# Opening and convolution of an S4 layer as one written list of single-engine steps: 24-step poles, loads on two queues, five forms of phase rounding

## The chip, the cores and the metric

The kernel runs on one core of a Trainium2 chip. A core has five engines that run their own instruction lists and wait for one another at semaphores: TensorE (PE, matrix products, results in PSUM), VectorE (DVE), ScalarE (ACT, functions from tables that must be loaded), GpSimd (POOL) and SyncE (SP). Transfers are started from an engine's list; here SP and POOL start nearly all of them. The metric is the device time of one execution in microseconds. The median of 3 runs of the kernel before is 1785.16 (1783.84 to 1787.31).

## The reference

One layer with a state-space convolution and one gated MLP, both modulated by a vector c; length 2048, 576 channels, 128 states per channel. Cut to what the change touches:

```
dt = exp(log_dt);  logdA = dt * (A_re + i A_im)
K[d, l] = Re sum_n C[d,n] * exp(logdA[d,n] * l) * dt*B[d,n]      # 2048 taps for 576 channels
y = (causal convolution of u with K over l) + u * Dskip
sa, ca, ga, sb, cb, gb = silu(c) @ w_mod
x = x + ga * y,   with u = layernorm(x) * (1 + ca) + sa
x = x + gb * mlp(layernorm(x) * (1 + cb) + sb)
```

## The kernel before

`body` (L120) calls `ssm` (L165), which does everything up to the first residual sum, then `phase_a` and `phase_b` of the MLP. The change is in `ssm`.

**Poles.** `poles` reads the seven pole arrays and computes decay, phase and amplitude of each pole; each is split into three bf16 parts and stored to `pa_d` and `pb_d` in DRAM. `p0` covers the first of four channel blocks (144 columns wide), `p1` the other three (432 wide). They are generators: each `next` issues one of seven pieces. `poles_load` reads a block back as the matmul operands `lb`, `lc`, `la` (two buffers each), from GpSimd's queue.

**Groups.** The kernel K is made in 36 groups of 16 channels, nine for each channel block. A group passes through

- `e_unit` (L444): exponents by matmul into PSUM (`ps` and `pk`), then ACT's Exp into `et` (L451, L454);
- `t_unit` (L458): phases in turns by matmul into a two-bank PSUM tile `ps` (L467), then the distance to the nearest whole turn into `ft`, and its absolute value (L484);
- `s_unit` (L487): ACT's sine of both, for cosine and sine (L489, L490);
- `p_unit` (L492): four products on DVE (L500 to L503);
- `kg_unit` and `k1_unit`: matmuls (L513, L530) and evacuations (L516, L535 on DVE, L537 on ACT).

Rounding has two forms. For groups under `NR = 10` PE adds a large constant and takes it off again by matmuls with constant rows of `sel`, and DVE copies the result out of PSUM (L479); for the others ACT adds the constant (L482) and DVE subtracts twice (L483):

```
if g < NR:  magics(2112, True); phases((768, 0), False, False)
            magics(2240, False); phases((1536, 1792), False, True)
            V.tensor_copy(f, pa)
else:       phases((768, 0), True, True)
            A.activation(f, pa, AF.Identity, bias=magic)
            V.scalar_tensor_tensor(f, f, MAGIC, pa, op0=ALU.subtract, op1=ALU.subtract)
```

PSUM holds two tiles `ps` of two banks (`ps2`, L182) and four tiles `pk` of one (`ps1`, L185). The first serve exponents, phases, modulation and layer norm; the others the rest.

**Layer norm and modulation.** `mod_unit` makes six rows from c and w_mod; `ln_load` brings x in four blocks into two buffers, `ln_stats` takes mean and variance (blocks 0 and 1 on ACT, 2 and 3 by bn_stats on DVE, L408), `ln_rows` and `ln_pair` normalise, take the first step of the transform over l, and store to `u1_d` by 16 transfers of GpSimd (L436).

**Convolution.** For each of five channel ranges: `u_unit` (transform, L580, and two transfers that swap halves, L582, L583), `z_unit` (kernel transform, L592, and product with u, L593), `v_unit` (inverse, L600 to L603, to `v_d`), `y_unit` (last inverse, residual sum and store, L646 to L649).

**What sets the order.** A loop over ticks 0 to 39 calls the units: in tick t group t makes its phases, t−1 its sines, t−2 its products, t−3 and t−4 the rest; exponents come for three groups in every third tick; the layer norm has ticks 0 to 7; pole reloads stand at ticks 7, 13 and 21; convolution steps are placed by the table `plan`. Within a queue the scheduler may reorder what the loop issues, except calls through `mlp.tied`, which stay in program order (L152 in the profile). The part behind the loop (L750 on: the last convolution steps beside the MLP's start) is written out by hand and pinned. Loads are on SP's queue; stores, swaps of u and pole reloads are on GpSimd's.

Of the kernel before, what the change touches and what calls it, by code (L numbers as in the profile page):

```python
# [18 lines left out]
D = 576  # L19
# [144 lines left out]

def ssm(tc, I, x1_d, consts_s, dram, mod_d, mlp):  # L165
    nc = tc.nc
# [4 lines left out]
    with ExitStack() as ctx:  # L171
# [24 lines left out]
        ep = early.enter_context(tc.tile_pool(name="ep", reuse_waits="tile", bufs=2, side="right"))  # L196


        def poles(c0, c1, Q, own=None):
            w = 144 * (c1 - c0)  # L200
            f0, f1 = CW * c0, CW * c1

            def t(n, dt=F32):
                return ep.tile([128, 432], dt, name="t_" + n, bufs=1)[:, :w]

            todo = []

            def split3(*items):

                n = 3 // (c1 - c0)  # L210
                parts = []
                for i, (src, dst, k) in enumerate(items):
                    if not todo:
                        t_ = ep.tile([128, 3, 432], BF, name="pt")
                        todo.extend(t_[:, :, w * j:w * j + w] for j in range(n))
                    parts.append((src, dst, k, todo.pop(0), t("sq%d" % (i % 2))))
                for src, dst, k, pt, q in parts:
# [3 lines left out]
                for src, dst, k, pt, q in parts:  # L221
                    V.tensor_tensor(pt[:, 2], q, pt[:, 1], op=ALU.subtract)
                    for c in range(c0, c1):
                        for h in range(2):
                            Q.dma_start(dst[c, h, k:k + 3].rearrange("q (p f) -> p q f", p=64),
                                        pt[64 * h:64 * h + 64, :, 144 * (c - c0):144 * (c - c0) + 144])

            nat = {}
            for n in ("log_dt", "A_im", "A_re", "C_re", "B_re", "C_im", "B_im"):
                nat[n] = t("n_" + n) if own is None else own[:, len(nat) * w:len(nat) * w + w]  # L230
                S.dma_start(nat[n].rearrange("p (c f) -> p c f", c=c1 - c0), I["A_" + n][f0:f1].rearrange("(c p f) -> p c f", p=128, f=144))

            def run():
                Cr, Ci, Br, Bi = nat["C_re"], nat["C_im"], nat["B_re"], nat["B_im"]
                wr, wi, q1, q2 = t("wr"), t("wi"), t("q1"), t("q2")
                ldt, dt, al, tau, tau64, rnd = nat["log_dt"], t("dt"), nat["A_re"], nat["A_im"], t("tau64"), t("rnd")
                A.activation(dt, ldt, AF.Exp)
                V.tensor_tensor(tau, dt, tau, op=ALU.mult)
                V.tensor_scalar(tau, tau, 1.0 / (2 * math.pi), 2097152.0, op0=ALU.mult, op1=ALU.min)
                V.tensor_scalar(tau, tau, -2097152.0, None, op0=ALU.max)  # L240
                V.tensor_scalar(rnd, tau, MAGIC, MAGIC, op0=ALU.add, op1=ALU.subtract)
                V.tensor_tensor(tau, tau, rnd, op=ALU.subtract)
                V.tensor_tensor(al, dt, al, op=ALU.mult)
                yield
                V.tensor_tensor(wr, Cr, Br, op=ALU.mult)
                V.tensor_tensor(wi, Ci, Br, op=ALU.mult)
                V.tensor_tensor(q1, Ci, Bi, op=ALU.mult)
                V.tensor_tensor(wr, wr, q1, op=ALU.subtract)
                V.tensor_tensor(q2, Cr, Bi, op=ALU.mult)
                V.tensor_tensor(wi, wi, q2, op=ALU.add)  # L250
                yield
                ax, ay, mx, mn, ph, lw = Cr, Ci, Br, Bi, t("ph"), t("lw")
                V.tensor_single_scalar(ax.bitcast(I32), wr.bitcast(I32), 0x7FFFFFFF, op=ALU.bitwise_and)
                V.tensor_single_scalar(ay.bitcast(I32), wi.bitcast(I32), 0x7FFFFFFF, op=ALU.bitwise_and)
                V.tensor_tensor(mx, ax, ay, op=ALU.max)
                V.tensor_tensor(mn, ax, ay, op=ALU.min)
                V.tensor_scalar(mx, mx, 1e-37, None, op0=ALU.max)
                V.reciprocal(rnd, mx)
                V.tensor_tensor(mn, mn, rnd, op=ALU.mult)
                yield  # L260
                A.activation(lw, mx, AF.Ln)
                AP = mlp.tied.scalar
                AP.activation(q1, mn, AF.Square)
                AP.activation(q1, q1, AF.Ln, bias=one)
                AP.activation(ph, mn, AF.Arctan)
                V.tensor_scalar(tau64, tau, 64.0, None, op0=ALU.mult)
                V.tensor_scalar(rnd, tau64, MAGIC, MAGIC, op0=ALU.add, op1=ALU.subtract)
                V.tensor_tensor(tau64, tau64, rnd, op=ALU.subtract)
                yield
                split3((al, pb_d, 0), (tau, pa_d, 0))  # L270
                yield
                V.scalar_tensor_tensor(lw, q1, 0.5, lw, op0=ALU.mult, op1=ALU.add)
                V.tensor_tensor(lw, lw, ldt, op=ALU.add)
                split3((tau64, pa_d, 3), (lw, pb_d, 3))
                yield
                V.tensor_scalar(ph, ph, 1.0 / (2 * math.pi), None, op0=ALU.mult)
                V.tensor_tensor(ax, ay, ax, op=ALU.is_gt)
                V.tensor_scalar(ay, ph, -2.0, 0.25, op0=ALU.mult, op1=ALU.add)
                V.tensor_tensor(ay, ay, ax, op=ALU.mult)
                V.tensor_tensor(ph, ph, ay, op=ALU.add)  # L280
                V.tensor_scalar(ay, ph, -2.0, 0.5, op0=ALU.mult, op1=ALU.add)
                V.scalar_tensor_tensor(ay, wr, 0.0, ay, op0=ALU.is_lt, op1=ALU.mult)
                V.tensor_tensor(ph, ph, ay, op=ALU.add)
                yield
                V.scalar_tensor_tensor(ay, wi, 0.0, ph, op0=ALU.is_lt, op1=ALU.mult)
                V.scalar_tensor_tensor(ph, ay, -2.0, ph, op0=ALU.mult, op1=ALU.add)
                V.scalar_tensor_tensor(ph, tau, 31.5, ph, op0=ALU.mult, op1=ALU.add)
                V.tensor_scalar(rnd, ph, MAGIC, MAGIC, op0=ALU.add, op1=ALU.subtract)
                V.tensor_tensor(ph, ph, rnd, op=ALU.subtract)
                split3((ph, pa_d, 6))  # L290

            return run()
# [3 lines left out]
        def poles_load(c, Q):  # L296
            for n, d_, k in (("lb", pb_d, 0), ("lc", pa_d, 0), ("la", pa_d, 3)):
                t_ = tb.tile([112, 9, 128], BF, name=n)
                if n == "lb":
                    Q.memset(t_[32:64], 0.0)  # L300
                for h in range(2):
                    Q.dma_start(t_[64 * h:64 * h + 48], d_[c, h, k:k + 6].rearrange("q (c g n) -> (q c) g n", c=8, g=9))
                lt[n, c] = t_
# [10 lines left out]

        def mod_init():
            A.activation(ec, cT, AF.Exp, scale=-1.0)
            V.tensor_scalar(ec, ec, 1.0, None, op0=ALU.add)
            V.reciprocal(ec, ec)
            V.tensor_tensor(ec, ec, cT, op=ALU.mult)

# [5 lines left out]
        def mod_load(k):  # L326
# [6 lines left out]
            for hh in range(2):  # L333
                S.dma_start(wmt[k][hh], I["w_mod"][:, k, hh])
# [5 lines left out]
        msk = cp.tile([128, 2], F32, name="msk")  # L340

        def mod_unit(k):
            wm = wmt.pop(k)
            mpart = ep.tile([128, D], F32, name="mpart", bufs=1)
            pm = ps2()
# [5 lines left out]
            A.activation(v3(mpart), pm[:, :, :HC], AF.Copy)  # L351
            pm = ps2()
            for hh in range(2):
                T.matmul(pm[:, hh, :HC], ones, mpart[:, HC * hh:HC * hh + HC], start=True, stop=True)
            src = pm[:, :, :HC]
            if k == 2:
                A.activation(v3(gar), src, AF.Copy)
            elif k == 1:
                V.scalar_tensor_tensor(v3(cga), src, 1.0, v3(gar), op0=ALU.add, op1=ALU.mult)
            elif k == 0:  # L360
                V.tensor_tensor(v3(sga), src, v3(gar), op=ALU.mult)
# [4 lines left out]
            else:  # L366
                mrow = ep.tile([128, D], F32, name="gar", bufs=1)
# [4 lines left out]
                G.dma_start(mod_d[k - 3:k - 2], mrow[0:1])  # L372


        x4s = {}
        r1t = {}

        def ln_load(i):
            x4s[i] = ep.tile([128, 4, D], F32, name="ln_x")
            S.dma_start(x4s[i], I["x"][:, 4 * i:4 * i + 4])  # L380
# [306 lines left out]
        for _ in range(3):  # L687
            next(p0)
# [1510 lines left out]
```

## Time and profile before

| | |
|---|---|
| median of 3 runs | 1785.16 us |
| span of the profiled execution | 1781.6 us |
| part of the span up to the end of the convolution | 456 us |
| PE, DVE, ACT, POOL busy, share of the span | 94%, 71%, 47%, 14% |
| first exponential on ACT begins | 46.41 us |
| last group's product on DVE ends | 381 us |
| last sum of the residual begins | 453.75 us |

Rows of the profile name a line of the kernel, an engine, an operation and "out<-in". In tables by stretch each engine has its busy microseconds in the stretch and a count of instructions; PEclk is the clock granted to TensorE as a share of the full one. In the timeline a row is start, duration, engine, line, operation, and in brackets the idle time before it and what ended it. In the chain of waits a row is start, length and what the end of the execution hung on then.

### The profile page before, as it was taken

The page shows a single profiled execution, that of the slowest core. Times are in us where ns is not written, and L with a number is a line of the kernel's source. Part 1 is how long each engine was busy: PE and PEld are TensorE (multiplying, and loading weights), DVE is VectorE, ACT ScalarE, POOL GpSimd, SP SyncE. Part 2 cuts the span into 40 slices and gives each one's busy share as a digit, 9 for nine tenths or more (in the row PEclk, how much of TensorE's full clock was granted, in tenths as well). Part 3 has the DMA queues.
Part 4 walks back from the last instruction along what each step waited for, and adds up shares of the span by engine and source line. Part 5 has one row for each costly group of instructions (what it writes and reads, how often), then busy time and mean ns, then how long its engine had stood idle before and what let it go on. Part 6 is the DMA issues. An engine that isn't in the chain of part 4 may idle for free.

```text
span 1781.6 us, 36375 instructions
## 1 busy us (share of the span) xinstructions
PE 1671.0 (94%) x15174; PEld 1242.2 (70%) x15174; DVE 1258.9 (71%) x2259; ACT 833.9 (47%) x1118; POOL 244.8 (14%) x400
## 2 busy tenths in 40 slices
PE   3687899997899999999999999999999999999999
PEld 1243555565455545777877888888888888888887
DVE  6874999965899998698899778688344478344432
ACT  4766998854477656445434444234232223122210
POOL 3312232333122211000000000000111100111100
PEclk9576999998899999999999999999999999999999
DMA  9456645579689879777675886874766573556531
GB/s 260 133 179 184 189 124 172 172 204 297 206 260 283 246 229 267 281 245 256 233 224 164 287 302 240 267 244 125 249 219 232 195 234 98 192 195 219 192 111 41
DMA packets 183381, 376.24 MB, mean 211 GB/s; under 512 B 39360, under 2 KB 103488, under 8 KB 182448
## 3 DMA queue, kind: packets, MB, share of 16 engines
q1 hardware_dynamic: 140416, 175.23, 32.7%
q0 software_dynamic: 36896, 172.01, 29.3%
q10 hardware_dynamic: 5904, 26.67, 3.7%
q8 instruction: 119, 1.95, 0.5%
q14 instruction: 46, 0.38, 0.1%
HBM read 263.11 MB, written 101.31 MB: 205 GB/s over the span
## 4 chain that ended last, share of the span: by engine, by line
PE 57%; DVE 16%; DMA 3%; issue 3%; ACT 1%; POOL 0%; ACTq 0%; SPq 0%; DVEq 0%; POOLq 0%
PE ps L152 54%; DVE bsz L152 2%; DVE zset L152 1%; DVE n L152 1%; DVE gt L152 1%; DVE rq L152 1%; DMA zset<-set_d 1%; DVE wsp L152 1%; DMA wsst<-in_w_spT 1%; DVE wso L152 1%; DVE nt L152 1%; DVE raw L152 1%; DVE rx L152 1%; DVE bsx L152 1%; DVE z L152 1%
## 5 line engine op out<-in xcount | busy, mean ns | idle before, releaser
L152 PEld LDWEIGHTS <-zset 128*128 128x128 f16 x7182 | 702.1, 98 | 91.9 <-DVE zset L152 7.6
L152 PE MATMUL ps<-wsp,zset 128*128 128x256 f16 x6048 | 667.4, 273 | 6.9 <-DVE zset L152 5.8
L152 PE MATMUL pz<-wz,nt 128*128 128x512 f16 (+1 forms) x1120 | 223.4, 360 | 8.9 <-DVE nt L152 4.2
L152 ACT ACTIVATE z<-gt 128x1024 f16<-128x1024 f32 x56 | 59.0, 1054 | 288.6 <-DVE gt L152 288.6
L152 PEld LDWEIGHTS <-nt 128*128 128x128 f16 x1120 | 109.9, 99 | 116.3 <-DVE nt L152 5.7
L152 DVE SCALAR_TENSOR_TENSOR gt<-ps,sc,bsp 128x512 f32<-128x512 f32 x36 | 27.0, 749 | 205.0 <-PE ps L152 203.3
L1907 POOL DMA_DIRECT2D zset<-set_d x96 | 50.8, 529 | 868.5 <-PE ps L152 614.6
L152 PE MATMUL ps<-wout,z 128*128 128x288 f16 x1344 | 170.0, 286 | 0.0
L152 PEld LDWEIGHTS <-z 128*128 128x128 f16 x1344 | 131.5, 98 | 33.0
L152 PE MATMUL ps<-n2o,zset 128*128 128x256 f16 x1134 | 128.2, 273 | 0.0
L152 DVE SCALAR_TENSOR_TENSOR gt<-ps,sc,gt 128x512 f32<-128x512 f32 (+1 forms) x180 | 122.2, 696 | 7.9 <-DVE gt L152 0.5
L152 DVE TENSOR_TENSOR raw<-raw 128x512 f32<-128x512 f32 (+2 forms) x228 | 119.1, 528 | 12.3 <-DMA raw<-z_d 7.9
L152 ACT ACTIVATE zset<-raw 128x1792 f16<-128x1792 f32 x48 | 81.0, 1690 | 57.8 <-PE ps L152 23.4
L152 DVE TENSOR_TENSOR zset<-raw,zset 128x1792 f16<-128x1792 f32 x48 | 96.9, 2019 | 14.9 <-ACT zset L152 14.9
L152 DVE TENSOR_TENSOR z<-ps,z 128x512 f32<-128x512 f32 (+1 forms) x126 | 71.9, 598 | 36.8 <-ACT z L152 26.7
L152 ACT ACTIVATE wsp<-raw,sc 128x1792 f16<-128x1792 f32 x25 | 44.6, 1785 | 43.0 <-DVE raw L152 35.3
L152 ACT ACTIVATE z<-z,sc 128x1024 f32<-128x1024 f32 x21 | 24.1, 1149 | 75.6 <-DVE z L152 71.9
L152 ACT ACTIVATE z<-pz,sc 128x512 f32<-128x512 f32 (+1 forms) x96 | 52.3, 579 | 15.0 <-PE pz L152 10.9
L152 PE MATMUL ps<-n2q,wf 128*128 128x512 f16 x252 | 55.7, 379 | 0.0
L152 ACT ACTIVATE z<-z,nm,r 128x1152 f32<-128x1152 f32 x24 | 31.5, 1343 | 50.3 <-DVE nm L152 28.2
L501 DVE TENSOR_TENSOR pg<-et,ft 128x1024 f32<-128x1024 f32 x36 | 43.8, 1217 | 13.3 <-ACT ft L489 11.6
L152 PE MATMUL ps<-wout,z1b 128*128 128x288 f16 x384 | 52.6, 286 | 0.5 <-ACT z1b L152 0.5
(358 smaller groups left out, 2461.9 us busy)
## 6 DMA issues: line engine op xcount, KB each, us to landing
zset<-set_d POOLq DMA_DIRECT2D x96, 896.0 KB, 4.9
raw<-z_d SPq DMA_DIRECT2D x48, 512.0 KB, 5.7
set_d<-zset ACTq DMA_DIRECT2D x24, 896.0 KB, 6.1
z_d<-z POOLq DMA_DIRECT2D x32, 576.0 KB, 9.2
zset<-wa_d POOLq DMA_DIRECT2D x18, 896.0 KB, 4.8
raw<-in_w_spT SPq DMA_DIRECT2D x25, 512.0 KB, 4.4
set_d<-zset SPq DMA_DIRECT2D x12, 896.0 KB, 5.9
u_d<-st1o POOLq DMA_DIRECT2D x16, 576.0 KB, 4.1
```

The source lines that it names most:

```text
L152: return self.tc.keep_in_program_order(f(*a, **k))
L501: V.tensor_tensor(pr, pi, c3[:, :, None, :].to_broadcast([128, 16, 2, 32]), op=ALU.mult)
L1907: self.nc.gpsimd.dma_start(o, self.set_d[f, j - 1] if j else self.wa_d[f])
```

## The change

`nc` in `ssm` is now `mlp.tied`, so that every instruction of the stage keeps the place in which it is written, on each engine. The units are cut into steps, as a rule of one engine each (`e_p` matmul, `e_a` exponential; `t_p` phases, `t_i` copy or added constant, `t_b` absolute value; `s_f`, `s_c` sines; `p_a`, `p_b`, `p_c` products; and so on), and one list calls them. The 24-piece poles, the layer norm's statistics (block 0 on ACT, blocks 1, 2 and 3 by bn_stats on DVE), the convolution and the hand-written part behind the loop are words of the same list. A table `GPQ` names 41 loads that go on GpSimd's queue; the rest stay on SP's. A table `MODE` gives each group's form of rounding, and `COPY` says for each group which engine evacuates `k1` (DVE 14 times; 13 before).

```diff
-    nc = tc.nc
+    nc = mlp.tied
+MODE = [int(k) for k in "333301130222221440204304000000000000"]
+COPY = "010001110000011111010000000100100011"
+ORDER = """
+pole_in.0.6 pole_in.0.5 pole_in.0.3 pole_in.0.0 pole_in.0.2 pole_in.0.4 pl.0.3 pole_in.0.1 pl.0.0 pole_in.1.1 pole_in.1.2 pole_in.1.5 load.c pl.0.4
...
+    def Q(*a):
+        return G if ".".join(str(k) for k in a) in GPQ else S
...
+    def t_p(g):
...
-            if g < NR:
+            if MODE[g]:
                 magics(2112, True)
                 phases((768, 0), False, False)
                 magics(2240, False)
                 phases((1536, 1792), False, True)
-                V.tensor_copy(f, pa)
             else:
                 phases((768, 0), True, True)
...
+    def t_i(g):
...
+        if MODE[g] == 0:
+            A.activation(cs[:, 1], pa, AF.Identity, bias=magic)
+        elif MODE[g] == 1:
+            V.tensor_copy(cs[:, 1], pa)
+        elif MODE[g] == 3:
+            A.activation(cs[:, 1], pa, AF.Copy)
...
+    def t_b(g):
...
+        if MODE[g] == 0:
+            V.scalar_tensor_tensor(cs[:, 1], cs[:, 1], MAGIC, pa, op0=ALU.subtract, op1=ALU.subtract)
+        src = pa if MODE[g] == 2 else cs[:, 1]
+        if MODE[g] == 4:
+            A.activation(cs[:, 0], pa, AF.Abs)
+        else:
+            V.tensor_single_scalar(cs[:, 0].bitcast(I32), src.bitcast(I32), 0x7FFFFFFF, op=ALU.bitwise_and)
...
+    def s_f(g):
...
+        A.activation(cs[:, 1], pa if MODE[g] in (2, 4) else cs[:, 1], AF.Sin, scale=-TWO_PI)
...
-        for tick in range(NG + 4):
+        for word in ORDER:
+            name, *a = word.split(".")
+            unit[name](*[int(k) if k.isdigit() else k or None for k in a])
```

By `MODE`, six groups have form 3 (0 to 3, 7, 21), three form 1 (5, 6, 14), six form 2 (9 to 13, 18), four form 4 (15, 16, 20, 23) and seventeen form 0 (4, 8, 17, 19, 22, 24 to 35). ACT loads a table 37 times in the stage; before, 32 times.

How the order moves, at three places. First GpSimd's list, from the poles' later stores to the first swaps of u (`u_d<-st1o` is a store of the layer norm, `lb<-pb_d` a pole reload). Before:

```order
L436 DMA u_d<-st1o 128x4x288 x2
L372 DMA mod_d<-gar 16x1x36
L436 DMA u_d<-st1o 128x4x288 x2
L372 DMA mod_d<-gar 16x1x36
L436 DMA u_d<-st1o 128x4x288 x6
L152 MEMSET lb 32x1152
L152 DMA lb<-pb_d 48x1152 x2
L152 DMA lc<-pa_d 48x1152 x2
L152 DMA la<-pa_d 48x1152 x2
```

Now:

```order
L152 DMA lc<-pa_d 48x1152 x2
L152 DMA mod_d<-gar 16x1x36
L152 DMA u_d<-st1o 128x4x288 x2
L152 DMA r1t<-in_c_r1t 128x128
L152 MEMSET lb 32x1152
L152 DMA lb<-pb_d 48x1152 x2
L152 DMA mod_d<-gar 16x1x36
L152 DMA u_d<-st1o 128x4x288 x2
L152 DMA mod_d<-gar 16x1x36
L152 DMA pa_d<-pt 64x3x144 x6
L152 DMA u_d<-st1o 128x4x288
L152 DMA la<-pa_d 48x1152 x2
```

The reload of `lb` stood behind all 16 stores of the layer norm; now eight of them follow it, and `lc` is earlier still. Next ACT's list in the middle of the groups, a batch of exponentials and what follows. Before (`ft<-ps,consts_s` is form 0's added constant, `ft<-ft` the sines):

```order
L451 ACT_TABLE_LOAD
L451 ACTIVATE et<-ps 128x1024
L454 ACTIVATE et<-pk 128x512
L451 ACTIVATE et<-ps 128x1024
L454 ACTIVATE et<-pk 128x512
L451 ACTIVATE et<-ps 128x1024
L454 ACTIVATE et<-pk 128x512
L482 ACTIVATE ft<-ps,consts_s 128x1024
L489 ACT_TABLE_LOAD
L489 ACTIVATE ft<-ft,consts_s 128x1024
L490 ACTIVATE ft<-ft 128x1024
```

Now, near the same place:

```order
L152 ACT_TABLE_LOAD
L152 ACTIVATE et<-ps 128x1024
L152 ACTIVATE kab<-pk 128x256
L152 ACTIVATE v<-pk 128x512
L152 ACTIVATE et<-ps 128x1024
L152 ACTIVATE et<-pk 128x512 x2
L152 ACTIVATE ft<-ps 128x1024
L152 ACTIVATE kab<-pk 128x256
L152 ACTIVATE et<-pk 128x512
L152 ACTIVATE ft<-ps,consts_s 128x1024
L152 ACT_TABLE_LOAD
L152 ACTIVATE ft<-ps 128x1024
```

Rows `ft<-ps` without `consts_s` are new: ACT's absolute value, copy or sine straight from PSUM, some of them on the far side of a table load from the group's other steps. Last, DVE's list from the last group product on (`pg` a product of a group, `zz` a convolution product, `xb` a residual sum, `k_` a k1 evacuation). Before:

```order
L501 TENSOR_TENSOR pg<-et,ft 128x1024
L502 SCALAR_TENSOR_TENSOR et<-ft,et 128x16x32
L503 TENSOR_TENSOR et<-ft,et 128x16x32
L593 TENSOR_TENSOR zz<-pk,uu 128x1024 x2
L520 TENSOR_TENSOR kab<-kab,dsk 128x4
L535 COPY k_4284<-pk 128x32x16
L648 TENSOR_TENSOR xb<-pk,xb 128x512
L593 TENSOR_TENSOR zz<-pk,uu 128x1024 x2
L520 TENSOR_TENSOR kab<-kab,dsk 128x4
L648 TENSOR_TENSOR xb<-pk,xb 128x512
L593 TENSOR_TENSOR zz<-pk,uu 128x1024 x2
```

Now:

```order
L152 TENSOR_TENSOR pg<-et,ft 128x1024 x2
L152 SCALAR_TENSOR_TENSOR et<-ft,et 128x16x32
L152 TENSOR_TENSOR et<-ft,et 128x16x32
L152 TENSOR_TENSOR kab<-kab,dsk 128x4 x2
L152 COPY k_4408<-pk 128x32x16
L152 MEMSET ones 128x128
L152 COPY k_4408<-pk 128x32x16
L152 TENSOR_TENSOR zz<-pk,uu 128x1024 x2
```

Ten convolution products were left behind the last group product, seven are now; the others, with their matmuls, stand among the groups.

More of the change, by code (lines that the diff above doesn't have):

```diff
@@ L196, in ssm, with step, pole_in @@
         ep = early.enter_context(tc.tile_pool(name="ep", reuse_waits="tile", bufs=2, side="right"))
-        def poles(c0, c1, Q, own=None):
+        unit = {}
+        def step(fn):
+            unit[fn.__name__] = fn
+            return fn
+        done = set()
+        def Q(*a):
+            return G if ".".join(str(k) for k in a) in GPQ else S
+        nat = {}
+        pole = {}
+        CQ = {0: (0, 1), 1: (1, 4)}
+        @step
+        def pole_in(i, k):
+            c0, c1 = CQ[i]
             w = 144 * (c1 - c0)
@@ L201, in poles @@
             f0, f1 = CW * c0, CW * c1
[L203 to L213, printed above, removed]
+            n = ("log_dt", "A_im", "A_re", "C_re", "B_re", "C_im", "B_im")[k]
+            if i == 0 and not nat:
+                nat["own"] = tb.tile([128, 1536], F32, name="et", bufs=5)
@@ L228, in poles @@
[L228 to L290, printed above, removed]
@@ L292, in poles @@
-            return run()
-        lt = {}
[L296 to L303, printed above, removed]
+                            o = 144 * (c - self.c0)
@@ new lines, in pl, with pload @@
+        @step
+        def pl(i, k):
+            if i not in pole:
+                pole[i] = Poles(i, G)
+            pole[i].run(k)
+            done.add(("pole", i, k))
+        lt = {}
+        @step
+        def pload(c, n):
+            assert all(("pole", min(c, 1), k) in done for k in ((12, 15), (12, 15), (15, 23))[n])
+            n, d_, k = (("lb", pb_d, 0), ("lc", pa_d, 0), ("la", pa_d, 3))[n]
+            t_ = tb.tile([112, 9, 128], BF, name=n)
+            if n == "lb":
+                G.memset(t_[32:64], 0.0)
+            for h in range(2):
+                G.dma_start(t_[64 * h:64 * h + 48], d_[c, h, k:k + 6].rearrange("q (c g n) -> (q c) g n", c=8, g=9))
+            lt[n, c] = t_
@@ new lines, in turn @@
+        @step
+        def turn():
+            assert all(("u1", b, h) in done for b in range(0, 16, 2) for h in range(2))
+            assert all(("mod", k) in done for k in range(6)) and ("pole", 1, 23) in done
+            early.close()
+            pools["cs"] = ctx.enter_context(tc.tile_pool(name="cs", reuse_waits="tile", bufs=1, side="right"))
+            pools["sb"] = ctx.enter_context(tc.tile_pool(name="sb", reuse_waits="tile", bufs=2, side="right"))
+            pools["wpre"] = ctx.enter_context(tc.tile_pool(name="wpre", reuse_waits="tile", bufs=2, side="right"))
@@ L600, in v_unit, with v_a, y_v @@
             T.matmul(pm, inva, zz[:, 0], start=True, stop=False)
             T.matmul(pm, invb, zz[:, 1], start=False, stop=True)
-            A.activation(v, pm, AF.Copy)
+        @step
+        def v_a(c, i):
+            v = half() if c == NC - 1 and i > 1 else part("v")
+            A.activation(v, st.pop(("vp", c, i)), AF.Copy)
             G.dma_start(v_d[c][:, kr(c, i)], by(v, c))
-        def y_vload(c, q):
+            done.add(("v", c, i))
+        @step
+        def y_v(c, q):
+            assert all(("v", c, i) in done for i in range(32 * CHW[c] // 512))
@@ L806, in ssm @@
[L806 to L824 removed]
+            done.add(("y", c, q))
@@ new lines, in end, with ml @@
+        @step
+        def end():
+            assert not tt and not et and not pw
+            tabs.close()
+        @step
+        def ml(name, *a):
+            mlp.nc = nc
+            if name == "start_x1":
+                assert all(("y", c, 0) in done for c in range(3))
+            if name == "sums":
+                mlp.start_sums(ps2(), ps2())
+                return
+            if name == "ap":
+                mlp.ap = mlp.wzp
+                return
+            getattr(mlp, name)(*a)
```

718 lines of the change are left out of this document (426 added, 292 removed).

## The prediction

> **What bounds the kernel now.** Every duration below is from one profiled execution:
>
> ```profile
> span 1781.6 us, 36375 instructions
> ```
>
> The page gives its span; the three timed runs of the same kernel have a median of 1785.16 us, so 3.6 us lie around the span. The sum is made on the span, and 3.6 is added at the end. Next I read busy time by stretch, with the cuts where the work changes its kind: loads and poles; the first groups beside the layer norm; groups 9 to 35; z, u, v and y steps; the last transfers; and the rest, which the change does not touch.
>
> ```profile
> core 0: us, PE busy (x) PEld busy (x) DVE busy (x) ACT busy (x) POOL busy (x), PEclk, DMA share, GB/s
> 0.00:46.00 46.00, 18.01 (x86) 6.79 (x86) 27.10 (x91) 21.39 (x45) 15.70 (x30) 0.91 0.97 259
> 46.00:183.00 137.00, 101.83 (x1344) 50.82 (x1343) 95.23 (x196) 94.80 (x139) 33.27 (x50) 0.68 0.56 168
> 183.00:381.00 198.00, 183.21 (x2648) 110.54 (x2648) 181.09 (x228) 177.60 (x236) 59.84 (x103) 0.98 0.58 165
> 381.00:430.00 49.00, 48.34 (x423) 31.21 (x421) 21.09 (x36) 19.57 (x27) 16.61 (x27) 1.00 0.98 273
> 430.00:456.00 26.00, 14.16 (x143) 11.33 (x140) 20.26 (x58) 9.02 (x12) 8.04 (x11) 0.67 0.96 287
> 456.00:1782.00 1326.00, 1305.46 (x10541) 1031.56 (x10538) 914.15 (x1654) 511.50 (x662) 111.36 (x180) 1.00 0.66 217
> ```
>
> In the second row nothing is full: PE works 101.8 of 137 us, DVE and ACT about 95. That is a stretch of waits, with 35 us of PE idle, and TensorE was granted only 0.68 of its clock. In the third row three engines are each 90 to 93% busy. In the fourth PE is the bound (48.3 of 49). The last row, 74% of the span, runs the same instructions in the same order after the change; nothing there is counted.
>
> Then the waits of the second row, in the timeline, of GpSimd, PE and DVE in turn:
>
> ```profile
> 156.89 0.75 POOL L436 DMA_DIRECT2D u_d<-st1o  x1 [1.43 <-ACT st1o L435]
> 157.63 1.08 POOL L152 MEMSET lb<- 32x1152 bf16 x1
> 159.00 1.31 POOL L152 DMA_DIRECT2D lb<-pb_d  x2 [0.29 <-POOL lb L152]
> 165.40 0.58 PE L450 MATMUL ps<-sel,lb 48*128 48x512 bf16 x1 [6.76 <-DMA lb<-pb_d]
> 176.13 1.23 DVE L479 COPY ft<-ps 128x1024 f32<-128x1024 f32 x1 [11.68 <-PE ps L467]
> 116.62 0.46 DVE L408 BATCH_NORM_STATS2 bs<-ln_x 128x6 f32<-128x288 f32 x1 [6.26 <-DMA ln_x<-in_x]
> ```
>
> The first four rows are one chain: the reload of the pole tables for groups 9 to 17 stands in GpSimd's queue behind the last store of the layer norm. So PE gets its first exponent matmul for those groups 6.76 us late, and DVE, which must round the phases that follow it, stands for 11.68. The sixth row is a second stall: DVE waits 6.26 us for a block of x.
>
> **The change part by part.**
>
> *The reload of lb.* It moves ahead of the layer norm's last eight stores, and in the listed order 24 steps ahead of its first reader. The wait was 11.68 on DVE. That it goes whole is one end; the other is nothing, if the memset ahead of the reload only waits for its buffer in the same place. I take −11.7, since two buffers exist and the first group block needs one. What is late next is PE's own work: PE's idle total of 35 is the end below which the stretch cannot shrink at this clock.
>
> *The block of x.* It is loaded further ahead of its statistics: −6.3, with 0 as the other end. The load of the block after it stands only four steps ahead of the statistics that read it, but several products of DVE stand between the matmuls that free its buffer and those statistics.
>
> *First exponential.* Here I take 0. It waits for three matrices of w_mod before and after; now the second block of x is loaded ahead of the last of them, 1.18 MB, which at 259 GB/s (first row) is 4.6 us later, while the poles' smaller steps let other work in. Ends −5 and +4.6. The 41 loads on GpSimd's queue cost POOL about 0.66 us each (half the reload's row, 1.31 for two): 27 us beside 33 and 60 busy of 137 and 198, hidden; if a uu transfer queues behind a load that waits for its buffer, its wait shows on DVE as L593 waiting for uu. Shared transfers run on the same engines: in the first row their share is 0.97 already, so a second queue brings no bytes.
>
> *Five forms of phase rounding.* The prices, from the groups of the third stretch by shape, and of the opening for the copy (L479, in the stretch 50 to 185):
>
> ```profile
> L483 DVE SCALAR_TENSOR_TENSOR ft<-ft,ps 128x1024 f32<-128x1024 f32 x25 | 30.3, 1213 | 8.5 <-ACT ft L482 8.4
> L482 ACT ACTIVATE ft<-ps,consts_s 128x1024 f32<-128x1024 f32 x25 | 28.6, 1146 | 0.9 <-PE ps L467 0.9
> L484 DVE TENSOR_SCALAR ft<-ft 128x1024 int32<-128x1024 int32 x25 | 17.1, 686 | 0.2
> L451 ACT ACT_TABLE_LOAD x8 | 10.3, 1283 | 0.1
> ```
> ```profile
> L479 DVE COPY ft<-ps 128x1024 f32<-128x1024 f32 x10 | 12.2, 1217 | 14.8 <-PE ps L467 14.8
> ```
>
> Forms 0 and 1 cost DVE 1.21 + 0.69 = 1.90 us. Form 4 costs it nothing (Abs goes to ACT in place of Identity). Form 3 leaves 0.69 (ACT copies). Form 2 is one AND that reads PSUM, which the trace does not show: between 0.69 (the same AND from SBUF) and 1.22 (a copy from PSUM); I take 1.22. From group 10 on: five groups of form 2 (10 to 13 and 18) save 3.4, four of form 4 save 7.6, one of form 3 saves 1.2: DVE −12.2, to 169 of 198. ACT loses Identity in six groups (form 2 and one of form 1), −6.9, and gains five table loads, 5 × 1.28 = +6.4: nothing. PE adds its rounding constants by two more pairs of matmuls in eleven of those groups. This is their price at full clock, from a pair of the same shape:
>
> ```profile
> 239.62 0.39 PE L450 MATMUL ps<-sel,lb 48*128 48x512 bf16 x2 [0.63 <-ACT et L451]
> ```
>
> 11 × 2 × 0.39 = +8.6 on PE. In the opening, form 3 takes five copies from DVE (−6.1), and the statistics of a block of x go from ACT to DVE (eight of 0.46, the row of 116.62, and their ends, about +4.5): both beside the waits, nothing.
>
> *Table loads by rule.* Two rows:
>
> ```profile
> 237.25 1.28 ACT L451 ACT_TABLE_LOAD   x1
> 238.54 1.02 ACT L451 ACTIVATE et<-ps 128x1024 f32<-128x1024 f32 x1
> ```
>
> The exponential begins 0.01 us after the load ends. The Trainium skill, "ScalarE: Activation LUTs", section "What ACT_TABLE_LOAD costs", puts a switch at about 1.28 us of load and 1.38 of drain, 2.66 together; by that five more would be an estimated 13.3 us of ACT. The rows show the load and no drain behind it, so the sum keeps 6.4.
>
> *Moved z, u and v.* Seven z products are left on DVE behind the last group product, against ten before. Their prices on PE, in the chain of waits:
>
> ```profile
> 389.99 1.98 PE pk L592 x16
> 391.98 0.86 PE pk L600 x2
> 392.84 0.86 PE pk L601 x2
> ...
> 396.44 1.91 PE pk L580 x4
> ```
>
> One step is half the first row, one pair of the next two, and half the last: 0.99 + 1.72 + 0.96 = 3.67, three are 11. This is work moved, not removed: what the tail loses, groups 9 to 35 must take. So both stretches are summed on PE, from 183 to 456: busy 183.2 + 48.3 + 14.2 = 245.7, plus 8.6 for rounding. Idle was 14.8 + 0.7 up to 430 and 11.8 behind it. The 11.8 stays, since the last transfers do:
>
> ```profile
> 430.47 5.49 DMA v_d<-uu
> ...
> 436.43 3.41 DMA uu<-v_d
> 439.88 3.36 PE pk L152 x31
> ...
> 444.05 5.94 DMA uu<-v_d
> ...
> 450.03 3.69 PE pk L152 x44
> ```
>
> Of the 15.5 I let a quarter stay, 4, because DVE has 12 us less to do and PE has steps to fill gaps with. 245.7 + 8.6 + 4 + 11.8 = 270.1 against 273: −3. Ends: +8.6 if all idle time stays, −7 if none does.
>
> **Sum.** −11.7 − 6.3 − 3 = −21: span 1760.6, with 3.6 around it **1764**.
>
> **The rivals.**
>
> *Deeper: the opening's clock rises too.* These rows are cuts of the second stretch:
>
> ```profile
> 99.00:119.00 20.00, 18.17 (x319) 10.32 (x315) 9.76 (x24) 13.50 (x23) 3.39 (x5) 1.00 0.89 258
> 119.00:130.00 11.00, 6.83 (x82) 3.15 (x86) 10.83 (x32) 3.39 (x4) 0.76 (x1) 0.53 0.33 116
> 160.00:177.00 17.00, 10.27 (x91) 4.45 (x93) 4.43 (x5) 7.92 (x11) 3.34 (x7) 0.51 0.83 222
> ```
>
> The grant is either about 0.5 or 1.0, and it is 1.0 where PE is nearly full (18.2 of 20) and halves in the two stretches with the stalls. If the stalls go, the 6.8 + 10.3 us of matmuls at half clock take 8.6 less. As much again in the stretch from 46 on, where 0.5 was granted too, and all idle of the middle filled (4 more): 1764 − 8.6 − 8.6 − 4 = 1743; below 1748 counts here. The Trainium skill, "TensorE: Matmul & The Clock Gate", section "What's actually happening", says the same as a rule: half clock after an idle window of about 3.4 us, full clock after one as long of sustained work. The three rows agree with it. Against this case: DVE and ACT have 95 of 137 to do, and ACT holds PE back as well.
>
> *Little or nothing.* The stalls are only passed on: with lb early, PE's half-clocked work and ACT's exponentials are late instead. Then −18 shrinks to 0 to −6 and −3 remains: 1776 to 1782. If the eleven magic groups also cost in full, 8.6 − 6, it is no change.
>
> *Slower: PSUM pairs held longer.* Phases lie in one of two pairs of banks, which exponentials, phases and layer norm share. In form 0 the pair is free when DVE has subtracted; in forms 2 and 4 only when ACT's sine has read it:
>
> ```profile
> 242.02 0.28 PE L467 MATMUL ps<-sel,lc 48*128 48x256 bf16 x2
> 243.90 1.22 DVE L483 SCALAR_TENSOR_TENSOR ft<-ft,ps 128x1024 f32<-128x1024 f32 x1 [2.13 <-ACT ft L482]
> 246.23 1.04 ACT L490 ACTIVATE ft<-ft 128x1024 f32<-128x1024 f32 x1
> ```
>
> Before: 242.02 to 245.12, 3.1 us. Held to the end of that group's sine: 247.27, 5.25, so 2.15 more; where ACT first does a batch of three exponentials (1.02 each, the row of 238.54) with two table loads (1.28), 5.6 on top of that. Ten groups, with each added microsecond passed on to PE, cost 21 to 78. It decides from 2.1 us per group on, where it has eaten the 21. At 4 us: +40 − 21 = +19, 1804. For it: table loads are more, and PE cannot run ahead in a pinned order. Against: the sines may be put early, and PE had 15 us of idle there.
>
> That the change does not do what it says is seen in no row: the lists of instructions differ as told.
>
> **How the numbers follow.** About 0.2%, 3.6 us, is what a measurement of this kernel can tell: no change is 1781.6 to 1788.7. Forecast, 1748 to 1776: 0.50. Deeper, below 1748: 0.21. Little, 1776 to 1781.6: 0.05. No change: 0.07. Slower: 0.17. So faster 0.76. The range leaves out a tenth or less on each side: 1733, ten below the deeper case's number, and 1796, where PSUM holding costs 3.2 us per group.
>
> **What would show it.** Before, the first exponential, a product of group 9 and the last group product stand here:
>
> ```profile
> 46.41 1.02 ACT L451 ACTIVATE et<-ps 128x1024 f32<-128x1024 f32 x1 [2.92 <-PE ps L152]
> ```
> ```profile
> 183.17 1.22 DVE L500 TENSOR_TENSOR pg<-et,ft 128x1024 f32<-128x1024 f32 x1
> ...
> 378.27 1.22 DVE L501 TENSOR_TENSOR pg<-et,ft 128x1024 f32<-128x1024 f32 x1
> ```
>
> Group 9's should come near 165, with no wait for lb or x of over 2 us ahead of it. The last should stand near 368, since 18 us are gone and three steps more lie ahead of it (11, less the 3 gained), and the final chain keep its 23 us from its first transfer to the last add. The AND from PSUM should take 1.2 us. If 46 to 165 shows a grant over 0.8, the deeper case is on. Waits of PE's matmuls into ps for ACT's sine, over 2 us a group, would make the forecast wrong; so would a first exponential behind 50.

## The result, and the profile after

Median of the changed kernel 1759.74 us (4 runs, 1755.47 to 1761.15), of the kernel before, timed beside it, 1786.24 (4 runs): ratio 0.9848, 95% interval 0.9831 to 0.9865. Forecast were 1764 and faster. The medians differ by 26.5 us. The profiled execution has a span of 1759.3 us, 22.3 less than before; 21 had been forecast on the span. It is one of the two longest of the four (1753.6 to 1759.3).

The same stretches as before, of the changed kernel:

```profile
core 0: us, PE busy (x) PEld busy (x) DVE busy (x) ACT busy (x) POOL busy (x), PEclk, DMA share, GB/s
0.00:46.00 46.00, 19.93 (x86) 7.22 (x87) 27.87 (x81) 22.25 (x47) 14.85 (x28) 1.00 0.84 233
46.00:183.00 137.00, 104.05 (x1557) 55.93 (x1555) 114.74 (x236) 110.66 (x150) 52.09 (x80) 0.76 0.63 191
183.00:381.00 198.00, 192.35 (x2761) 117.78 (x2760) 164.38 (x203) 169.93 (x228) 77.77 (x126) 1.00 0.66 189
381.00:430.00 49.00, 40.08 (x305) 29.05 (x306) 32.26 (x82) 18.43 (x22) 18.06 (x27) 0.83 0.87 264
430.00:456.00 26.00, 19.72 (x101) 9.53 (x100) 23.13 (x65) 13.53 (x17) 1.95 (x4) 1.00 0.59 191
```

The second row now holds 20 us more DVE work and 16 more ACT work in the same 137 us. Cut where PE fills up, it shows more:

```profile
46.00:160.00 114.00, 81.05 (x1225) 42.40 (x1223) 96.05 (x213) 91.31 (x125) 40.03 (x61) 0.72 0.60 187
160.00:360.00 200.00, 199.91 (x2878) 121.45 (x2878) 173.60 (x213) 180.43 (x240) 79.87 (x132) 1.00 0.65 186
```

The kernel before, in the same two stretches:

```profile
46.00:160.00 114.00, 86.12 (x1149) 42.90 (x1147) 86.83 (x186) 81.75 (x124) 29.93 (x44) 0.69 0.50 155
160.00:360.00 200.00, 179.13 (x2529) 105.25 (x2531) 170.53 (x213) 176.49 (x231) 56.42 (x98) 0.94 0.60 171
```

From 160 us on PE has no idle time for 200 us (before, 179.1 of the same 200). DVE and ACT are 87 and 90% busy beside it. Three milestones in the timeline, against 46.41, 183.17 and 378.27 before: the first exponential, the tenth group's pair of products and the last group's (a row of x2 starts with the first of the two).

```profile
42.87 1.02 ACT L152 ACTIVATE et<-ps 128x1024 f32<-128x1024 f32 x1
```
```profile
164.27 2.35 DVE L152 TENSOR_TENSOR pg<-et,ft 128x1024 f32<-128x1024 f32 x2
...
361.94 2.36 DVE L152 TENSOR_TENSOR pg<-et,ft 128x1024 f32<-128x1024 f32 x2
...
428.15 0.42 DVE L152 TENSOR_TENSOR x1l<-pk,x1l 128x256 f32<-128x256 f32 x1 [0.41 <-PE pk L152]
```

The last row is the last residual sum, 453.75 before. All runs in one table: us at which, in the profiled execution, the first exponential begins, the tenth and the last group's first product end, the last residual sum begins; then the span, and the timed ratio to the kernel before.

| run | first exp. | tenth group | last group | last sum | span | ratio (95%) |
|---|---|---|---|---|---|---|
| before | 46.4 | 183.3 | 378.3 | 453.8 | 1781.6 | 1 |
| changed | 42.9 | 165.5 | 363.2 | 428.2 | 1759.3 | 0.9848 (0.9831 to 0.9865) |
| before + lb early | 43.8 | 169.9 | 366.7 | 441.6 | 1772.3 | 0.9948 (0.9934 to 0.9963) |
| before + x early | 44.4 | 179.6 | 374.7 | 450.1 | 1780.6 | 0.9999 (0.9985 to 1.0013) |
| before + forms | 47.5 | 178.6 | 384.7 | 460.8 | 1790.1 | 1.0029 (1.0016 to 1.0042) |
| changed, lb late | 43.6 | 170.0 | 367.1 | 432.3 | 1760.8 | 0.9870 (0.9854 to 0.9887) |
| changed, forms of before | 43.5 | 168.2 | 389.5 | 454.7 | 1783.3 | 1.0017 (1.0005 to 1.0029) |
| changed, form 0 from group 10 | 43.2 | 163.5 | 384.8 | 449.9 | 1782.9 | 0.9998 (0.9985 to 1.0011) |
| changed, one load queue | 49.9 | 171.7 | 372.4 | 435.4 | 1763.8 | 0.9903 (0.9885 to 0.9920) |
| changed, y step later | 43.6 | 166.2 | 364.2 | 426.3 | 1753.2 | 0.9855 (0.9838 to 0.9872) |
| changed, not pinned | 49.8 | 167.3 | 394.6 | 464.9 | 1797.1 | 1.0100 (1.0072 to 1.0127) |
| changed, no form 4 | 42.1 | 168.3 | 380.7 | 443.3 | 1775.4 | 0.9954 (0.9936 to 0.9972) |
| changed, no form 2 | 44.0 | 166.5 | 368.4 | 432.9 | 1766.0 | 0.9899 (0.9876 to 0.9921) |
| changed, u twice | 44.2 | 162.4 | 367.4 | 432.9 | 1763.6 | 0.9902 (0.9882 to 0.9922) |

How far such numbers can be read: behind the last sum all runs do the same work, and it takes them 1326.9 to 1333.1 us. So a span differs by up to 3 us either way for reasons of its own, and the milestones of the stage are the better measure of a step. They scatter too: the first exponential differs by 3.7 us (43.8 to 47.5) among the four kernels in the old order, two of which run the same program throughout and the others up to there. The tenth group stands between 162.4 and 168.3 in four executions in the new order whose programs are alike up to it (changed, y step later, no form 4, u twice).

### The profile page after: what moved, and what is told of

It reads as the page before. It is cut to its first block, busy times and chain, and to the rows that moved or that the text cites. A ratio compares the mean times of both kernels' runs of the same rounds, so it can differ in the third digit from the quotient of the medians.

```text
span 1759.3 us, 36489 instructions
## 1 busy us (share of the span) xinstructions
PE 1661.2 (94%) x15246; PEld 1240.5 (71%) x15246; DVE 1253.8 (71%) x2254; ACT 832.4 (47%) x1107; POOL 275.0 (16%) x442
## 5 line engine op out<-in xcount | busy, mean ns | idle before, releaser
L152 PE MATMUL pz<-wz,nt 128*128 128x512 f16 (+1 forms) x1120 | 222.1, 358 | 10.8 <-DVE nt L152 4.3
L152 DVE TENSOR_TENSOR zset<-raw,zset 128x1792 f16<-128x1792 f32 x48 | 96.9, 2019 | 16.2 <-ACT zset L152 16.1
L152 DVE TENSOR_TENSOR pg<-et,ft 128x1024 f32<-128x1024 f32 x72 | 85.5, 1218 | 3.3 <-PE pk L152 2.0
L152 PE MATMUL pk<-zz,small 128*128 128x512 f32 x144 | 70.1, 613 | 0.0
L152 ACT ACTIVATE wsp<-raw,sc 128x1792 f16<-128x1792 f32 x25 | 44.6, 1785 | 42.7 <-DVE raw L152 35.0
L152 DVE TENSOR_TENSOR zz<-pk,uu 128x1024 f32<-128x1024 f32 x36 | 44.0, 1221 | 19.8 <-PE pk L152 18.9
```

Of the source, the lines that this page charges most:

```text
L152: return self.tc.keep_in_program_order(f(*a, **k))
```

## The experiments

**The reload of lb, alone, in the kernel before.**

```diff
-            if tick in (7, 13, 21):
+            if tick in (5, 13, 21):
```

> The kernel before with one edit: the reload of the pole tables for groups 9 to 17 stands at tick 5 instead of 7, ahead of the last four stores of the layer norm. Theory (the stall is on the path): PE's 6.8 us wait for lb goes, group 9's products come 8 to 12 us earlier than 183.2, and the span falls by as much, 1770 to 1774. Rival (the stall is only passed on, to PE's half-clocked matmuls and ACT's exponentials): group 9's products come 0 to 4 us earlier, span 1778 to 1782.

The wait of PE for lb is gone, and the tenth group's second product begins here (183.17 before):

```profile
169.78 1.22 DVE L500 TENSOR_TENSOR pg<-et,ft 128x1024 f32<-128x1024 f32 x1
```

That is 13.4 earlier, of which 2.6 were there already at the first group's product (65.6 against 68.2): 10.8, with 11.7 forecast for the term. The ratio gives 9.3 us of 1785, and against the run below, a repeat of the kernel before, the tenth group is 9.8 earlier. The stall was on the path.

**The block of x ahead of two small loads, in the kernel before.** `ln_load` is called ahead of `r1_load` in ticks 1 and 3.

> The kernel before with one edit: in ticks 1 and 3 the next block of x is put on SP's queue ahead of the two small constant loads that it stood behind. Theory (each stall counts): the 6.3 us wait of DVE for x goes, span 1775 to 1777. Rival (the block waits for its buffer in any case, or DVE catches up later): the wait stays or the span is 1780 to 1783.

```profile
111.48 1.18 DVE L408 BATCH_NORM_STATS2 bs<-ln_x 128x6 f32<-128x288 f32 x3 [4.01 <-DMA ln_x<-in_x]
```

The edit changed nothing that ran. The scheduler puts the block back behind the two small loads, and the trace shows every engine's list in the order of the kernel before. One row of PE and three of SP's queue in this run:

```profile
102.76 0.71 PE L433 MATMUL ps<-ln_x,rt 32*64 32x288 f32 x13
98.66 0.35 SPq L384 DMA_DIRECT2D r1t<-in_c_r1t  x1
103.52 0.35 SPq L385 DMA_DIRECT2D cs<-in_c_cs  x1
103.96 1.44 SPq L380 DMA_DIRECT2D ln_x<-in_x  x1
```

So the theory was not tested, and the run is a repeat of the kernel before: its wait for x is 4.0 where it was 6.3 (and 4.15 in the run above), its tenth group comes 3.7 earlier, the time is the same. The rows show how little the place in the queue could give. There are two buffers for x, and the last matmul that reads the block two before ends at 103.47; the load starts 0.5 later. In the changed kernel it also starts 0.5 after that matmul (98.91 and 99.37), but DVE has other work until it reads the block at 116.71, and does not wait. What 6.3 us less of this wait would be worth was not settled.

**The forms alone, in the kernel before.** `MODE` replaces `g < NR`, and each group's steps follow it; loop, scheduler and queues are as before.

> The kernel before, same loop and scheduler, with the new table of rounding forms (and nothing else of the change). Theory (forms trade DVE time for PE time, near nothing): span within 5 us of 1781.6. Rival 1 (phases in PSUM held until the sine has read them stall PE): a loss of 20 us or more. Rival 2 (the forms are the gain): 1772 or less.

Slower by 5 us (0.29%). From the tenth to the last group it takes 206.1 us against 195.0, 11.1 more; the tenth group came 4.7 earlier, at a granted clock of 0.90 against 0.69 between 46 and 160. PE's extra matmuls, forecast at 8.6, were paid, and nothing came back for them from DVE and ACT: between 183 and 381 DVE's group products wait 19.6 us for PE, against 4.7 before.

**lb late again, in the changed kernel.** `pload.1.0` goes behind `turn`, that is behind the last store of the layer norm, with the steps that read it.

> The changed kernel with the reload of lb for groups 9 to 17 put back behind the last store of the layer norm, and the three exponent matmuls and two exponentials that stood ahead of that moved behind it. Theory (the early reload is most of the opening's gain): PE waits for lb again, for 5 us or more, and the span grows by 5 to 12 us, to 1764 to 1771. Rival (the gain is in the order as a whole, which has other work to do meanwhile): the span grows by less than 3 us.

```profile
152.54 1.44 PE L152 MATMUL pk<-sel,lb 112*128 112x512 bf16 x3 [6.86 <-DMA lb<-pb_d]
```

PE waits 6.9 us as before the change, yet the tenth group comes only 4.5 later, the last sum 4.1, and the span grows by 1.5, as the rival had it. The ratio's interval overlaps with that of the changed kernel, and 170.0 for the tenth group is 1.7 behind the latest of the four executions told above. So the early reload is worth some 4 us in the new list, not clear of the scatter, against 9 to 11 in the old. The trace shows one reason: with lb early, PE stands at nearly the same place for the layer norm's u instead, a wait that the run with lb late does not have there.

```profile
156.97 3.75 PE L152 MATMUL pk<-u,small 128*128 128x512 f32 x4 [4.84 <-DMA u<-u_d]
```

**The forms of before, in the new list.** `MODE` is ten times 1 and 26 times 0; in a second run only the groups from 10 on are set to 0.

> The changed kernel with the rounding forms of before (form 1 for groups 0 to 9, form 0 for the others) in the new order. Theory (PE is full from 160 to 373 us, so PE's extra matmuls for rounding are paid in full): 4 to 9 us less than the changed kernel's span of 1759.3, after up to 4 us more in the opening for DVE's copies. Rival (the forms take from DVE and ACT what the order needs them for): 3 to 15 us more.

> The changed kernel with form 0 for all groups from 10 on; groups 0 to 9 keep their new forms. Theory (PE is the bound there): the 11 pairs of pairs of rounding matmuls, 8.6 us, come off, span 1750 to 1753. Rival (DVE's 12 us more and ACT's 7 put them in PE's place): the span is 1759 to 1768 and PE has idle time between 183 and 360, where it has none now.

Both lose the whole gain. In the second run the tenth group is as early as in the changed kernel (163.5), and from there to the last group it takes 221.3 us against 197.7. Its busy time and its waits (line waited for: us in total, times, longest):

```profile
160.00:360.00 200.00, 179.01 (x2528) 107.90 (x2524) 165.69 (x203) 166.97 (x220) 70.78 (x115) 0.96 0.56 165
```
```profile
DVE ft L152 <- ACT ft L152: 11.1, 7, 3.3
ACT ft L152 <- DVE ft L152: 6.5, 3, 3.3
ACT ft L152 <- DVE et L152: 2.8, 1, 2.8
```

No engine is full: PE 179 of 200, DVE 166, ACT 167. So it is not busy time. DVE stands for ACT's added constant, then ACT stands for DVE's absolute value: 17.6 us between 160 and 300, against 1.4 of the first kind and none listed of the second in the changed kernel:

```profile
DVE ft L152 <- ACT ft L152: 1.4, 2, 1.1
```

It reaches PE: between 160 and 360 PE waits 21.0 us, the longest times for evacuations by ACT and DVE, and the changed kernel lists no wait of PE there.

```profile
PE pk L152 <- ACT kab L152: 4.9, 1, 4.9
PE pk L152 <- DVE k L152: 3.7, 1, 3.7
```

Both theories that were put down priced busy time, and both fail: the first by its sign, the second since the loss is larger than told and no engine took PE's place. One rival stays open: no run places the steps anew for form 0. So the loss belongs to these forms in this order; an order made for the old forms may lose less.

**One load queue.** The table `GPQ` is empty.

> The changed kernel with all loads on SP's queue (the table of 41 loads for GpSimd's queue is empty). Theory (the same engines carry both queues, issue is hidden): span within 3 us of 1759.3. Rival (loads that wait for a buffer hold back those behind them in one queue): 5 us more or worse, with new waits for x, u or w_mod.

The first exponential begins 7.0 us later, and all milestones up to the last sum are 6 to 9 later. The span, 4.5 longer, lies between the theory and the rival; by the ratio it is 9.8. The first 30 us of the changed kernel and of this one:

```profile
0.00:30.00 30.00, 9.25 (x50) 3.00 (x51) 16.95 (x63) 11.96 (x27) 7.38 (x16) 1.00 0.96 273
```
```profile
0.00:30.00 30.00, 4.26 (x24) 1.22 (x24) 15.72 (x58) 11.31 (x25) 3.94 (x10) 1.00 0.92 236
```

Two queues moved 273 GB/s there, one 236; up to 46 us it was 233 against 223. The first matrix of w_mod is used at 19.3 with two queues, where the wait before it ends with a step of DVE. With one it is used at 22.8, and the wait ends with the transfer:

```profile
22.75 2.13 PE L152 MATMUL ps<-wm,ec 96*32 96x288 f32 x12 [22.75 <-DMA wm<-in_w_mod]
```

**The y step that PE waits for.** `y_p.1.2` goes from behind `z_m.3.5` to behind `z_p.3.4`. In the changed kernel PE stands here, with steps of z and v behind it:

```profile
381.83 0.66 PE L152 MATMUL pk<-u,st 128*64 128x128 f32 x2 [6.39 <-DMA u<-v_d]
```

> The changed kernel with one matmul step of the last inverse (y_p.1.2) moved from ahead of five steps of z and v to behind them; PE now waits 6.4 us there for its reload from v_d, with the others queued behind. Theory (that wait is on the path to the last transfers): the last add comes 4 to 6 us earlier than 428.2, span 1753 to 1756. Rival (the end hangs on the transfers to and from v_d in any case): the last add comes 0 to 2 us earlier.

```profile
382.09 0.41 PE L152 MATMUL pk<-u,st 128*64 128x128 f32 x2 [0.18 <-DMA u<-v_d]
383.86 1.96 PE L152 MATMUL pk<-u,st 128*64 128x128 f32 x30 [1.36 <-DMA u<-v_d]
387.71 1.10 PE L152 MATMUL pk<-u,small 128*128 128x512 f32 x2 [1.89 <-DMA u<-u_d]
390.48 1.95 PE L152 MATMUL pk<-zz,small 128*128 128x512 f32 x4 [1.67 <-DVE zz L152]
```

The wait is cut up rather than gone: 0.2, 1.4, 1.9 and 1.7, for reloads of v and u and for DVE. The last sum comes 1.8 earlier, as the rival had it, and the ratio is the same. Three of the four waits are for transfers, so the end of the stage hangs on them in the main. The lower span (1753.2) came behind the stage and is within the scatter told above.

**Not pinned.** `nc` in `ssm` is `tc.nc` again; list, forms and queues stay.

> The changed kernel with its list, forms and queues, but the scheduler may reorder the instructions of the stage again, as in the kernel before. Theory (the list's gain needs the pinned order): PE is no longer full from 160 to 373 us and most of the 22 us is lost, span 1772 to 1785. Rival (forms, queues and the rough order do it, pins or not): span 1755 to 1764.

Slower than the kernel before, and by more than the theory's range. The tenth group is nearly as early (167.3), but then the scheduler pulls exponentials and sines out of their batches. Table loads on ACT between 46 and 400 us, by the line of the function that follows:

```profile
L657 ACT ACT_TABLE_LOAD x17 | 21.8, 1283 | 0.3
L721 ACT ACT_TABLE_LOAD x15 | 19.2, 1283 | 0.3
L728 ACT ACT_TABLE_LOAD x10 | 12.8, 1283 | 2.9 <-DVE ft L713 2.8
L659 ACT ACT_TABLE_LOAD x8 | 10.3, 1283 | 0.1
L369 ACT ACT_TABLE_LOAD x1 | 1.3, 1283 | 0.0
```

51, against 32 in the changed kernel: 19 × 1.28 = 24 us of ACT, on an engine that was 90% busy. From the tenth to the last group it takes 227.3 us against 197.7, 29.6 more. The loads are large enough to be most of that; they were not separated from the other changes of order.

**Form 4 and form 2, each replaced by form 0.** Groups 15, 16, 20 and 23 in one run, groups 10 to 13 and 18 in the other.

> The changed kernel with form 0 in place of form 4 for the four groups 15, 16, 20 and 23. Theory (in a fixed list form 0's trips ACT to DVE to ACT make both stand, so each form-4 group saves a trip of some 2 to 3 us): span 6 to 14 us over 1759.3, with more of ACT's ft waiting for DVE's and the other way round. Rival (only busy time counts: PE 3 us less, DVE 8 more): span within 3 us.

> The changed kernel with form 0 in place of form 2 for the five groups 10, 11, 12, 13 and 18. Theory (form 0's trips between ACT and DVE): span 6 to 14 us over 1759.3; with the run without form 4 it should come near the 24 us of the run without both. Rival (only busy time counts: PE 4 us less, ACT 6 and DVE 3 more): span within 3 us.

From the tenth to the last group: 212.4 and 201.9 us against 197.7, so 14.7 for four groups of form 4 and 4.2 for five of form 2; with both gone, and groups 14 and 21 changed too, it was 23.6. Without form 4 PE waits 11.3 us for ACT and DVE between 160 and 360, where it has no wait in the changed kernel, and ACT's sine stands for DVE's rounding:

```profile
205.73 1.15 ACT L152 ACTIVATE ft<-ft,consts_s 128x1024 f32<-128x1024 f32 x1 [3.29 <-DVE ft L152]
```

Form 4, in which DVE has no part, is worth most: 3.7 us a group in this order, twice the 1.9 of DVE's busy time that it saves, and by the span (16.1 more) past the theory's 14. Form 2's share is 4.7 us by the last sum and 6.7 by the span, at the lower edge of the theory's 6 to 14.

**PE's work added to.** The first matmul of the eight u steps of the second channel range is issued twice.

> The changed kernel with the first matmul of the eight u steps of the second channel range issued twice, same result: 8 x 0.87 = 7.0 us more for PE between 225 and 300 us and nothing for anyone else. Theory (PE alone is the bound there): the last group product comes 6 to 8 us later than 363.2 and the span grows by 5 to 8. Rival (PE is full but others set the pace too, and it catches up): less than 3 us.

From the tenth to the last group 205.0 us against 197.7: 7.3 for 7.0 us of work. PE's time is paid one for one there in the changed kernel; two runs with no work added in this stretch, y step later and lb late, take 198.0 and 197.1. Against the clock of the changed kernel the last group's product is only 4.2 later and the span 4.3 longer, less than the 6 to 8 and 5 to 8 of the theory, because this execution was 3.1 ahead at the tenth group. The opening, where its program is still that of the changed kernel, ran at another clock:

```profile
46.00:160.00 114.00, 82.39 (x1256) 42.78 (x1258) 97.93 (x216) 93.07 (x127) 40.44 (x63) 0.91 0.62 191
```

0.91 was granted against 0.72, and the tenth group came at 162.4 against 165.5: 3.1 us.

## Why the prediction was right, point by point

- **The bound before** was read rightly: waits in the opening, PE close behind DVE and ACT from group 9 on, transfers at the end.
- **The opening, −18 for two stalls.** The tenth group came 17.8 earlier, but not by this account. The lb term is nearly right in the old order (10.8 of 11.7, 9.3 by the ratio). In the new list some 4.5 of the 17.8 hang on it, and that is not clear of the scatter. Between 46 and 165 no wait of DVE for x is left and none of PE for lb, as foretold, but what the x term was worth no run shows; the kernel before itself waits 4.0 or 6.3 for x, from one execution to the next. Two queues, priced at nothing, are worth 6 to 7 from the first exponential on. The remainder was not taken apart; the rows show that DVE and ACT did 96 and 91 us of work by 160 where they had done 87 and 82.
- **"A second queue brings no bytes"** is the step that failed outright: 236 GB/s with one, 273 with two, in the first 30 us.
- **The forms, +8.6 on PE and −12.2 on DVE.** The AND from PSUM, taken at 1.22, measured 1.22. The 8.6 on PE is near what the trace shows, by luck: it counts four more matmuls per group, the constants, but a second set of phases comes with them, so there are eight (15246 matmuls against 15158 with form 0 from group 10 on: 88 for eleven groups). Set against that, a matmul starts before the one ahead of it has ended, so the rows' durations count too much. One group's rounding:

```profile
209.99 0.39 PE L152 MATMUL ps<-sel 48*128 48x512 bf16 x2
210.21 0.27 PE L152 MATMUL ps<-sel,lc 48*128 48x256 bf16 x2
210.32 0.27 PE L152 MATMUL ps<-sel,la 48*128 48x256 bf16 x2
210.43 0.38 PE L152 MATMUL ps<-sel 48*128 48x512 bf16 x2
210.65 0.27 PE L152 MATMUL ps<-sel,lc 48*128 48x256 bf16 x2
210.76 0.27 PE L152 MATMUL ps<-sel,la 48*128 48x256 bf16 x2
```

  From the first start to that of the next work (210.96) it is 0.97 us; form 0's phases take 0.23 (204.99 to 205.22). The difference, 0.74, is 8.1 for eleven groups; by durations the eight matmuls would be 14.5. Missing was a third price, that of the trips between ACT and DVE: in a list that cannot be reordered each engine stands for the other, and PE in the end for both. Without forms 4 and 2 (and the forms of groups 14 and 21) the new list takes 24 us longer; in the old order, where the scheduler placed the steps, the whole table of forms cost 5.
- **Middle and tail together, −3.** From the tenth group's product to the last sum it took 262.7 us against 270.5: −7.8, just past the end of this term's range, −7. The step that was mis-sized is the quarter of PE's idle time that was left: up to 360 none is left. Ten of the eleven us moved out of the tail: from the last group to the last sum 65.0 against 75.5. They came at 2.7 in the middle, where 8 were allowed.
- **Table loads.** Five more were priced at 6.4 by the rows; the gap behind a load is still 0.0 (53.01 + 1.28, then the next at 54.30). What many more of them go with was seen without pins.
- **The rivals.** "Deeper" had its condition, a grant over 0.8, in one execution of the changed kernel's opening, and there the tenth group came 3 us earlier, not 17: PE at a lower clock was not alone on the path. The run with the forms of before had 0.87 there and its tenth group at 168.2. "Slower", by phases held in PSUM, did not come: PE has no idle time from 160 to 360, though ten groups hold a pair until the sine.

So the total is in part luck: the queues and the tail gave more than was told, the early reload less, and these errors cancelled. The order as a whole, in which PE no longer waits, is the part that the sum had not priced. By the last sum the gain was 25.6; 3.3 of it are missing in the span, and that much differs between executions behind the stage.

## What to carry to other kernels

Undoing one part at a time (the early reload, the second queue, the forms from group 10 on, the pins) lost 4, 7, 22 and 37 us by the last sum, of a gain of 26: parts of a written order don't add up, since each was placed for the others. Price a step in a fixed list by the trips between engines that it makes as well as by its busy time: a rounding that takes 1.9 us of DVE cost 3.7 in this order, and the engines were seen to stand for each other. When the engine that bounds a stage is full, test that by giving it more work: 7.0 us more cost 7.3. That less work for it gains as much does not follow: form 0 takes 8 us off PE, and the list lost 22.

## What the runs showed of the hardware

With two issuing queues more was moved in the first 30 us, 273 against 236 GB/s, although with one the transfer engines were already 0.92 busy. With two they were 0.96 busy, so most of the difference is more bytes per busy microsecond. In that stretch the queues of the changed kernel (queue, kind: packets, MB, share of 16 engines) read

```profile
q1 hardware_dynamic: 4286, 6.17, 75.4%
q0 software_dynamic: 468, 2.01, 20.5%
```

so a packet of GpSimd's queue (q0) held 4.3 KB on average and one of SP's 1.4, and with all loads on SP's there were 5245 packets for 7.09 MB in place of 4755 for 8.19. The Trainium skill, "DMA: Bandwidth & Descriptors", section "Issuing engines are not separate DMA queues", says that a second issuer saves only the time of issuing. This case does not agree: SP reached the load of w_mod at the same time in both runs:

```profile
11.18 0.85 SPq L152 DMA_DIRECT2D wm<-in_w_mod  x2
```
```profile
11.24 1.12 SPq L152 DMA_DIRECT2D wm<-in_w_mod  x2
```

and yet the first matrix was used 3.5 us sooner with two. The table also changes which loads stand ahead of which; whether packet size or order makes the difference was not tried.

The granted clock between 46 and 160 us was 0.91, 0.72, 0.70 and 0.66 in four executions whose programs differ only later (u twice, changed, y step later, no form 4), with PE busy 81 to 83 us in each, and the tenth group came at 162.4, 165.5, 166.2 and 168.3. So neither the program nor PE's busy time alone settles the grant, and 0.25 of the clock goes with about 6 us there.
